# Five small reorderings of banks, copies and products in a chunked-attention and bilinear-FFN kernel

## The chip, the cores and the metric

One core of one Trainium2 chip. The time is the device time of one execution in microseconds (us).

The engines are named as the profile names them: PE (TensorE matmuls), PEld (its weight loads, beside PE), DVE (VectorE), ACT (ScalarE), POOL (GpSimd), and SP, whose queue issues most transfers. A "bank" is one of the PSUM areas into which PE writes; the kernel calls them pa, pb, pc, po, pq and pt.

## The reference, cut to what matters

```python
# q, k, v: 8 batches, 8 heads, 576 rows, 64 columns; attention within chunks of 64 rows
scores = scale * q_c @ k_c.T ; attn = softmax(scores) ; out = attn @ v_c
x = out as [4608 tokens, 512]
a = x @ w_a                       # 512 x 1536
b = x @ w_b
result = (a * b) @ w_out          # 1536 x 512
```

The kernel handles the tokens in 18 units of 256, two to a block of 512. A unit is cast, transposed, scored, summed and multiplied with v; a block of x then goes through the two products and the last one. The two products of blocks 0 and 1, and block 0's last one, are done plainly; all others are done by a scheme with seven products for eight, whose arithmetic the change does not touch.

## The kernel before

The transposes of unit 2 (`U == 2`): q and k get one bank each, and DVE and ACT each copy one half of every bank.

```python
t = [bank() for _ in range(2 if U < 2 else 1)]
tp = [t[i % len(t)]....[:, i] for i in range(2)]
...                                           # 4 transposes into tp[0], 4 into tp[1]
for i in range(2):
    on_dve = i == 0 if U in (0, 2) else w == 0 or U == 1
    cp = nc.vector.tensor_copy if on_dve else nc.scalar.copy
    cp(out=dst[:, i], in_=tp[i]...)
```

Block 0 goes in six pairs of column groups. Unit 2's parts are threaded into pairs 4 and 5:

```python
for i in range(NWP):                          # 6 pairs
    pair.b_of(0, ...)                         # 4 products with w_b, ACT copies the bank
    if i == 5: sums(2, halves=True)           # row sums; ACT: ln, exp(-), twice
    pair.b_of(1, ...)
    if i == 4: transpose_pe(2)
    pair.a_of(0)                              # 4 products with w_a, DVE multiplies
    if i == 4: scores(2)
    if i == 5: values(2)                      # attn @ v, DVE multiplies by 1/sum -> xT
    ...
    pair.a_of(1)
```

Block 1 then goes in half blocks `h()` that alternate between the bank pairs (pa, pc) and (pq, po), with unit 3's values after nine of them:

```python
values(3)          # 2 DVE multiplies
bring(6)
h(8)
...
for p in range(3):
    out_part(0, 2, p, psum_q)                 # third output tile of block 0
```

The tail has the last block's output in two groups (`th` 0 and 1), whose sum C lay in po and pa, and whose last product was cut in two halves:

```python
ends = [OutGroup(NBLK - 1, 0, (psum_t, psum_q, psum_o)),
        OutGroup(NBLK - 1, 1, (psum_t, psum_b, psum_a))]
...
for cols in (slice(0, 128), slice(128, 256)) if end else [slice(0, 256)]:
    for kt in range(HFT):
        nc.tensor.matmul(...)                 # 6 products
    if end:
        nc.vector.tensor_scalar(...)          # evict these columns
        store(..., nc.scalar if cols.start else nc.sync)
```

The softmax here doesn't subtract the row's maximum and nothing guards it: scores larger than these inputs give would overflow.

Of the kernel before, what the change touches and what calls it, by code (L numbers as in the profile page):

```python
# [16 lines left out]
def kernel(  # L17
# [28 lines left out]
    NBLK = NTOK // BLK  # L46
# [20 lines left out]
    psum_b = [psum_b0, psum_b1]  # L67
    psum_c = ctx.enter_context(tc.tile_pool(name="psumc", bufs=1, space=PSUM))
    psum_o = ctx.enter_context(tc.tile_pool(name="psumo", bufs=1, space=PSUM))
    psum_q = ctx.enter_context(tc.tile_pool(name="psumq", bufs=1, space=PSUM))  # L70
    psum_t = ctx.enter_context(tc.tile_pool(name="psumt", bufs=2, space=PSUM))
# [16 lines left out]
    def bank(pool=None):  # L88
        if pool is None:
            pool = spread[0]  # L90
            spread.append(spread.pop(0))
        if pool is psum_b:
            pool = psum_b[0]
            psum_b.append(psum_b.pop(0))
        return pool.tile([128, 512], FP32, name=bank_names[id(pool)])
# [133 lines left out]
    def transpose_pe(U, names="qk"):  # L229
        if U not in qkt:  # L230
            qkt[U] = qkt_pool.tile([128, 2, 2, NKT, 128], BF16, name="qkt")
        for n in names:
            w = "qk".index(n)
            src = raw.pop((n, U))
            t = [bank() for _ in range(2 if U < 2 else 1)]
            tp = [
                t[i % len(t)].bitcast(BF16).rearrange("c (i m p) -> c i m p", i=2, m=NKT)[:, i]
                for i in range(2)
            ]
            for i in range(2):  # L240
                for m in range(NKT):
                    nc.tensor.transpose(
                        tp[i][:, m, :],
                        src[:, i, 2 * m:2 * m + 2, :].rearrange("p j d -> p (j d)"),
                        identity,
                    )
            dst = qkt[U][:, w].rearrange("c g m (p i) -> c i m g p", i=2)
# [3 lines that stand above are left out]
                cp(out=dst[:, i], in_=tp[i].rearrange("c m (g p) -> c m g p", g=2))  # L251
# [17 lines left out]
    late = []  # L269
# [56 lines left out]
                out=rs_of[U][:, c], in_=ln_of[U][:, c], func=AF.Exp, scale=-1.0  # L326
            )

    def values(U, pools=(None, None)):
        E, rs, vr = E_of.pop(U), rs_of.pop(U), raw.pop(("v", U))  # L330
        K, u = divmod(U, 2)
        if u == 0:
            x_tiles[K] = x_pool.tile([128, NKT, BLK], FP16, name="xT")
        av = [bank(p).rearrange("p (m g s) -> p m g s", m=NKT, g=2) for p in pools]
        for m in range(NKT):
            for g in range(2):
                for cl in range(2):
                    for j in range(2):
                        nc.tensor.matmul(  # L339
                            av[cl][j * 64:j * 64 + 64, m, g, :],  # L340
                            vr[cl * 64:cl * 64 + 64, g, 2 * m + j, :],
                            E[cl * 64:cl * 64 + 64, j, m, g, :],
                            start=True,
                            stop=True,
                        )
        for cl in range(2):
            x = x_tiles[K][:, :, 256 * u:256 * u + 256]
            for m in (slice(0, 2), slice(2, 4)) if (U, cl) == (1, 1) else [slice(0, 4)]:
                nc.vector.tensor_tensor(
                    out=x.rearrange("p m (g c s) -> p m g c s", g=2, c=2)[:, m, :, cl, :],  # L350
                    in0=av[cl][:, m],
                    in1=rs[:, cl, m].rearrange("p m (g s) -> p m g s", g=2),
                    op=MULT,
                )

    def slot(s=None, f=None):

        if s is not None and s >= NU:
            s = None
        if f is not None:  # L360
            sums(f)
            inverse(f)
        if s is not None:
            scores(s)
        if f is not None:
            values(f)
# [48 lines left out]
    def ab_half(n, ft, u, t, whole=False):  # L415
        i, o = divmod(ft * 128, WCOL)
        c = slice(0, BLK) if whole else slice(256 * u, 256 * u + 256)
        for kt in range(NKT):
            nc.tensor.matmul(  # L419
                t[:, c],  # L420
                w_ab[n, i][:, kt, o:o + 128],
                x_tiles[0][:, kt, c],
                start=(kt == 0),
                stop=(kt == NKT - 1),
            )

    class Pair:
# [3 lines left out]
            self.fts = (2 * i, 2 * i + 1)  # L431
            self.b, self.b_sb = {}, {}

        def b_of(self, n, halves=(None,)):
            ft = self.fts[n]
            for u in halves:
                if ft not in self.b:
                    self.b[ft] = bank(psum_b)
                ab_half("wb", ft, u, self.b[ft], u is None)
            if halves[-1] == 0:  # L440
                return
            self.b_sb[ft] = c_pool.tile(
                [128, BLK], FP32, name=("b_sb", "u_sb", "v_sb", "c_sb")[ft % 4]
            )
            nc.scalar.copy(out=self.b_sb[ft], in_=self.b[ft])
# [137 lines left out]
    class OutGroup:  # L583
# [20 lines left out]
        def part(self, n, th):  # L604
# [7 lines left out]
            halves = lambda t: t if one else t.rearrange("p (h n) -> p h n", h=2)  # L612
# [7 lines left out]
            if n:  # L620
                s1, s2 = so_of[self.K, "s124"]
            t, a, w = (
                lambda: (self.A, a11, b11),
                lambda: (self.A, a12, b21),
                lambda: (self.B, s2, t2),
                lambda: (self.B, s1, t1),
                lambda: (self.C, s3, t3),
                lambda: (self.B, so_of[self.K, "s4"], b22),
                lambda: (self.C, a22, t4),
            )[n]()  # L630
            c0 = 0 if one else th * 256
            end = n == 6 and one and th == 1
            for cols in (slice(0, 128), slice(128, 256)) if end else [slice(0, 256)]:
                for kt in range(HFT):
                    nc.tensor.matmul(  # L635
                        t[:, c0:c0 + 256][:, cols],
                        a[:, kt, th * 128:th * 128 + 128],
                        w[:, kt, cols],
                        start=n in (0, 4) and first and kt == 0,
                        stop=last and kt == HFT - 1,  # L640
                        skip_group_check=True,
                    )
                if end:
                    nc.vector.tensor_scalar(
                        out=rows(self.o1, cols), in0=self.C[:, cols], scalar1=OUT_SCALE,
                        scalar2=None, op0=MULT,
                    )
                    store(
                        self.K, 1, th, self.o1[:, th], cols, nc.scalar if cols.start else nc.sync
                    )  # L650
# [53 lines left out]
    def out_part(K, tg, part, pool):  # L704
        if part == 0:
            out_ps[K, tg] = bank(pool)
        for ft in range(4 * part, 4 * part + 4):
            nc.tensor.matmul(  # L708
                out_ps[K, tg],
                ab_tiles[K][:, ft, tg * 128:tg * 128 + 128],  # L710
                wo_sb[:, ft],
                start=(ft == 0),
                stop=(ft == NFT - 1),
            )
        if part == 2:
            out_tile(K, tg, out_ps.pop((K, tg)))

    with tc.manual_schedule(
# [75 lines left out]

        for i in range(NWP):
            pair = Pair(i) if i else first
            pair.b_of(0, (None,) if i else (1,))
            if i == 5:
                sums(2, halves=True)
            pair.b_of(1, (None,) if i else (1,))  # L800
            if i == 4:
                transpose_pe(2)
            pair.a_of(0)
            if i == 4:
                scores(2)
            if i == 5:
                values(2)
            if 1 <= i < 5:
                combo()
            pair.a_of(1)  # L810
            if 0 <= i < 5:
                combo()
# [24 lines left out]
        halves = [(ft, u) for u in range(2) for ft in range(NFT)]  # L837

        def h(n=1):
            for _ in range(n):  # L840
                half(*halves.pop(0))
# [14 lines left out]
        h(1)  # L856
        inverse(3, 1)
        h(1)
        values(3)
        bring(6)  # L860
        h(8)
        out_0(0)
        transpose_pe(4)
        h(2)
# [20 lines left out]
        h(1)  # L885
        inverse(5)
        for p in range(3):
            out_part(0, 2, p, psum_q)
        spread[:] = [psum_t]
        values(5)  # L890
        h(1)
# [17 lines left out]
        for K in range(2, NBLK):  # L909
            U = 2 * K + 2  # L910
# [36 lines left out]
        for K in range(2, NBLK):  # L947
# [41 lines left out]
                now.p7()  # L989
                last = now  # L990
        ends = [
            OutGroup(NBLK - 1, 0, (psum_t, psum_q, psum_o)),
            OutGroup(NBLK - 1, 1, (psum_t, psum_b, psum_a)),
        ]
        last.add7()
# [42 lines left out]
```

## Time and profile before

| | before |
|---|---|
| median of 6 runs | 303.72 us (303.65 to 305.45) |
| span in the profile | 301.6 us |
| PE busy | 97% |
| PE's waits that the change aims at | six, 2.3 us by the profile |

The profile lists each engine's waits with what ended them. As PE is the bound, only its own waits matter. They are shown and read in the prediction, which was written from three runs, with a median of 303.73 us.

### The profile page before, as it was taken

What the parts mean: (1) busy time and instruction counts of PE and PEld (TensorE: products, weight loads), DVE (VectorE), ACT (ScalarE), POOL (GpSimd) and SP (SyncE); (2) the same over time, 40 slices, a digit from 0 to 9 for tenths busy, and PEclk for the clock granted to TensorE, in tenths of its full rate; (3) what the DMA queues carried; (4) which work ended last, traced back from release to release, by engine and by line L of the source; (5) the groups of instructions that cost most, each with busy time, mean ns of one, the idle gap of its engine ahead of it and who ended that gap; (6) DMA issues with size and microseconds to landing.
All of it is one profiled execution on the core that took longest, in us unless ns stands there. A gap on an engine that the chain in (4) does not pass through costs nothing.

```text
span 301.6 us, 8619 instructions
## 1 busy us (share of the span) xinstructions
PE 291.5 (97%) x3529; PEld 232.8 (77%) x3531; DVE 213.4 (71%) x344; ACT 197.5 (65%) x358; POOL 192.0 (64%) x179
## 2 busy tenths in 40 slices
PE   6799899999999999999999999999999999999995
PEld 2454468765688888888888888888888888888884
DVE  3548766857977696679667866795679577965773
ACT  2843567358587768776877687767776786566622
POOL 0557668999998299817971797179727902780650
PEclk9999999999999999999999999999999999999999
DMA  7999999999999999899869486947723001100024
GB/s 229 319 381 358 298 306 366 256 206 210 257 243 183 207 194 264 181 214 220 185 155 206 160 183 153 238 134 180 124 67 89 5 2 70 73 3 0 2 106 172
DMA packets 141159, 54.29 MB, mean 180 GB/s; under 512 B 117184, under 2 KB 135232, under 8 KB 141120
## 3 DMA queue, kind: packets, MB, share of 16 engines
q1 hardware_dynamic: 140976, 53.69, 71.0%
q8 instruction: 27, 0.44, 0.6%
q14 instruction: 12, 0.10, 0.1%
q10 hardware_dynamic: 144, 0.07, 0.1%
HBM read 37.75 MB, written 9.44 MB: 156 GB/s over the span
## 4 chain that ended last, share of the span: by engine, by line
PE 90%; ACT 4%; DVE 3%; DMA 2%; issue 1%; SPq 0%; DVEq 0%
PE pb L492 19%; PE pc L492 12%; PE pa L492 12%; PE po L635 12%; PE pq L635 10%; PE pb L419 3%; PE pb L708 3%; PE pa L401 2%; PE po L401 2%; PE pq L401 2%; PE pt L339 2%; PE pt L306 2%; DMA st<-in_k_dram 2%; PE pc L401 2%; PE po L419 1%; PE pc L419 1%
## 5 line engine op out<-in xcount | busy, mean ns | idle before, releaser
L572 POOL TENSOR_TENSOR so<-ab_sb 128x512 f16<-128x512 f16 x23 | 27.6, 1198 | 69.3 <-DVE ab_sb L542 69.3
L492 PEld LDWEIGHTS <-t 128*128 128x128 f16 x504 | 48.3, 98 | 8.5 <-issue 1.7
L492 PE MATMUL pb<-s,wa 128*128 128x256 f16 x336 | 50.5, 273 | 0.0
L492 PE MATMUL pa<-xT,wb 128*128 128x256 f16 x336 | 50.4, 273 | 0.0
L530 DVE TENSOR_TENSOR c_sb<-pc,v_sb 128x512 f32<-128x512 f32 x42 | 28.9, 688 | 26.9 <-ACT v_sb L503 25.6
L635 PEld LDWEIGHTS <-ab_sb 128*128 128x128 f16 x390 | 37.8, 98 | 5.2 <-issue 0.9
L492 PEld LDWEIGHTS <-wb 128*128 128x128 f16 x336 | 32.9, 98 | 4.0
L492 PEld LDWEIGHTS <-wa 128*128 128x128 f16 x336 | 31.8, 98 | 4.2 <-issue 0.2
L542 DVE SCALAR_TENSOR_TENSOR ab_sb<-pc,c_sb 128x512 f16<-128x512 f32 x42 | 29.0, 690 | 7.9 <-PE pc L492 6.5
L503 ACT COPY u_sb<-pb 128x512 f32<-128x512 f32 x42 | 24.7, 588 | 14.8 <-PE pb L492 14.7
L542 DVE SCALAR_TENSOR_TENSOR ab_sb<-pb,b_sb 128x512 f16<-128x512 f32 x42 | 28.9, 689 | 6.1 <-PE pb L492 5.2
L510 ACT COPY pb<-pa 128x512 f32<-128x512 f32 x42 | 24.0, 573 | 10.3 <-PE pa L492 9.9
L635 PEld LDWEIGHTS <-so 128*128 128x128 f16 x288 | 28.1, 98 | 3.4
L503 ACT COPY b_sb<-pa 128x512 f32<-128x512 f32 x42 | 25.0, 595 | 7.1 <-PE pa L492 7.1
L531 DVE TENSOR_TENSOR pc<-pc,u_sb 128x512 f32<-128x512 f32 x42 | 28.9, 688 | 0.0
L572 POOL TENSOR_TENSOR so<-so,ab_sb 128x512 f16<-128x512 f16 x23 | 27.2, 1184 | 1.7
L503 ACT COPY v_sb<-pb 128x512 f32<-128x512 f32 x42 | 24.7, 587 | 5.0 <-PE pb L492 4.4
L572 POOL TENSOR_TENSOR ab_sb<-ab_sb 128x512 f16<-128x512 f16 x23 | 26.8, 1165 | 0.0
L572 POOL TENSOR_TENSOR so<-ab_sb,so 128x512 f16<-128x512 f16 x23 | 26.3, 1174 | 0.0
L492 PE MATMUL pb<-s,t 128*128 128x256 f16 x168 | 25.3, 273 | 0.0
L492 PE MATMUL pc<-xT,t 128*128 128x256 f16 x168 | 25.2, 272 | 0.1
L492 PE MATMUL pc<-s,t 128*128 128x256 f16 x168 | 25.2, 273 | 0.0
(140 smaller groups left out, 570.9 us busy)
## 6 DMA issues: line engine op xcount, KB each, us to landing
st<-in_v_dram SPq DMA_DIRECT2D x32, 256.0 KB, 4.4
out_dram<-o_sb SPq DMA_DIRECT2D x30, 256.0 KB, 2.3
st<-in_k_dram SPq DMA_DIRECT2D x22, 256.0 KB, 4.6
st<-in_q_dram SPq DMA_DIRECT2D x20, 256.0 KB, 3.5
st<-in_q_dram SPq DMA_DIRECT2D x6, 512.0 KB, 6.0
st<-in_moe_w_b_dram SPq DMA_DIRECT2D x6, 512.0 KB, 7.4
st<-in_moe_w_a_dram SPq DMA_DIRECT2D x6, 512.0 KB, 6.7
st<-in_moe_w_out_dram SPq DMA_DIRECT2D x6, 512.0 KB, 6.6
```

Source lines behind the costliest of these rows:

```text
L306: nc.tensor.matmul(sm[cl][j * 64:j * 64 + 64, :], ones[cl * 64:cl * 64 + 64, :], E[cl * 64:cl * 64 + 64, j].rearrange("p m g s -> p (m g s)"),
L401: nc.tensor.matmul(ps[n], w_ab[n, i][:, kt, o:o + 128], xT[:, kt, c0:c1], start=(kt == 0), stop=(kt == NKT - 1),)
L419: nc.tensor.matmul(t[:, c], w_ab[n, i][:, kt, o:o + 128], x_tiles[0][:, kt, c], start=(kt == 0), stop=(kt == NKT - 1),)
L492: nc.tensor.matmul(t[:, h * 256:h * 256 + 256], w[:, kt, h * 128:h * 128 + 128], x[:, kt], start=start and h == 0 and kt == 0, stop=h == 1 ...
L503: nc.scalar.copy(out=t, in_=src)
L510: nc.scalar.copy(out=self.B, in_=self.A)
L530: nc.vector.tensor_tensor(out=self.c, in0=self.C, in1=self.v, op=ADD)
L531: nc.vector.tensor_tensor(out=self.C, in0=self.C, in1=self.u, op=ADD)
L542: nc.vector.scalar_tensor_tensor(out=self.dst[:, :, c0:c0 + 256], in0=t.rearrange("p (h n) -> p h n", h=2), scalar=AB_SCALE, in1=o.rearran ...
L572: (eng or nc.gpsimd).tensor_tensor(out=o, in0=x0, in1=x1, op=op)
L635: nc.tensor.matmul(t[:, c0:c0 + 256][:, cols], a[:, kt, th * 128:th * 128 + 128], w[:, kt, cols], start=n in (0, 4) and first and kt == 0, ...
L708: nc.tensor.matmul(out_ps[K, tg], ab_tiles[K][:, ft, tg * 128:tg * 128 + 128], wo_sb[:, ft], start=(ft == 0), stop=(ft == NFT - 1),)
```

## The change

Five places where PE waits are rearranged; not one product is added or removed. The diff, cut:

```diff
-            t = [bank() for _ in range(2 if U < 2 else 1)]
+            t = [bank() for _ in range(2 if U < 3 else 1)]
...
+            if later is not None and cl == 1:          # in values()
+                later.append(lambda: normalize(slice(0, 4)))
...
-            pair.b_of(0, (None,) if i else (1,))
+            pair.b_of(0, (None,) if i else (1,), i == 5)     # late: no copy yet
...
+            if i == 5:
+                values(2)
+                pair.copy(0)
+                pair.copy(1)
             pair.a_of(0)
...
-        values(3)
+        second = []
+        values(3, later=second)
         bring(6)
-        h(8)
+        h(1)
+        second.pop()()
+        h(7)
...
-            out_part(0, 2, p, psum_q)
+            out_part(0, 2, p, psum_b)
...
-            OutGroup(NBLK - 1, 0, (psum_t, psum_q, psum_o)),
+            OutGroup(NBLK - 1, 0, (psum_t, psum_q, psum_c)),
...
+            for cols in (slice(0, 128), slice(128, 256)) if end else []:
                 if end:                                # evictions after all 12 products
```

More of the change, by code (lines that the diff above doesn't have):

```diff
@@ L327, in inverse, with values @@
             )
-    def values(U, pools=(None, None)):
+    def values(U, pools=(None, None), later=None):
         E, rs, vr = E_of.pop(U), rs_of.pop(U), raw.pop(("v", U))
@@ L347, in values, with normalize @@
             x = x_tiles[K][:, :, 256 * u:256 * u + 256]
-            for m in (slice(0, 2), slice(2, 4)) if (U, cl) == (1, 1) else [slice(0, 4)]:
+            def normalize(m, cl=cl):
                 nc.vector.tensor_tensor(
@@ L354, in values @@
                 )
+            if later is not None and cl == 1:
+                later.append(lambda: normalize(slice(0, 4)))
+            elif (U, cl) == (1, 1):
+                normalize(slice(0, 2))
+                normalize(slice(2, 4))
+            else:
+                normalize(slice(0, 4))
     def slot(s=None, f=None):
@@ L432, in __init__, with b_of @@
             self.b, self.b_sb = {}, {}
-        def b_of(self, n, halves=(None,)):
+        def b_of(self, n, halves=(None,), late=False):
             ft = self.fts[n]
@@ L439, in b_of, with copy @@
                 ab_half("wb", ft, u, self.b[ft], u is None)
-            if halves[-1] == 0:
-                return
+            if halves[-1] != 0 and not late:
+                self.copy(n)
+        def copy(self, n):
+            ft = self.fts[n]
             self.b_sb[ft] = c_pool.tile(
@@ L796 @@
             pair = Pair(i) if i else first
-            pair.b_of(0, (None,) if i else (1,))
+            pair.b_of(0, (None,) if i else (1,), i == 5)
             if i == 5:
                 sums(2, halves=True)
-            pair.b_of(1, (None,) if i else (1,))
+            pair.b_of(1, (None,) if i else (1,), i == 5)
             if i == 4:
                 transpose_pe(2)
+            if i == 5:
+                values(2)
+                pair.copy(0)
+                pair.copy(1)
             pair.a_of(0)
@@ L805 @@
                 scores(2)
-            if i == 5:
-                values(2)
             if 1 <= i < 5:
```

## The prediction

> **What bounds the kernel now.** I read the page first. Its first two parts say that the TensorE is the bound nearly everywhere, at an undisturbed clock.
>
> ```profile
> PE 291.5 (97%) x3529; PEld 232.8 (77%) x3531; DVE 213.4 (71%) x344; ACT 197.5 (65%) x358; POOL 192.0 (64%) x179
> PEclk9999999999999999999999999999999999999999
> PE 90%; ACT 4%; DVE 3%; DMA 2%; issue 1%; SPq 0%; DVEq 0%
> ```
>
> PE is busy for 291.5 of 301.6 us, and 90% of the chain that ended last is PE work. No product is removed by this change, so it can only win where PE stands still. The second view is the list of PE's own waits over the whole span. I leave out those before 18 us, where the first units start and the change touches nothing.
>
> ```profile
> PE pa L279 <- ACT qkt L251: 0.9, 1, 0.9
> ...
> PE pa L635 <- DVE o_sb L644: 0.4, 1, 0.4
> PE pq L401 <- ACT o_sb L699: 0.3, 1, 0.3
> PE pa L401 <- DVE xT L349: 0.3, 1, 0.3
> PE po L635 <- DVE o_sb L676: 0.2, 1, 0.2
> PE po L401 <- DVE ab_sb L410: 0.2, 1, 0.2
> ```
>
> Each of these six occurs once, and each is the target of one edit. Together they are 2.3 us, or 0.8% of 303.73 us. These figures run from one modelled matmul end to the next start, so they understate: a group of four 256-column products issues every 0.44 us but is shown as 0.60 us. I therefore size each stall below from start times. Between 77 and 290 us the list has no PE wait of 0.2 us or more. That matters for whether an early gain survives.
>
> The third view is the timeline at the largest stall, the transposes of unit 2:
>
> ```profile
> 32.54 1.35 DVE L251 COPY qkt<-pt 128x512 bf16<-128x512 bf16 x2 [0.28 <-PE pt L242]
> ...
> 33.31 1.35 ACT L251 COPY qkt<-pt 128x512 bf16<-128x512 bf16 x2 [0.63 <-DVE qkt L251]
> ```
>
> q and k each have one bank, of which DVE copies one half and ACT the other. ACT stood still for 0.63 us until DVE had finished with q's bank, although both only read it. The scores of unit 2 started at 34.71, after ACT's last copy.
>
> **What the Trainium skill says.** "PSUM — Partial Sum Buffer", section "PSUM bank collisions raise a hardware error", says that two engines may not be in one bank and quadrant at once, two readers included, so access is to be guarded by bank. The trace agrees with the effect: the 0.63 us above. For unit 0, which has two banks, DVE's copy ran 7.34 to 8.06 and ACT's 7.52 to 8.25, side by side. In the tail PE likewise waits for DVE's eviction of columns that it doesn't write. The same page, section "Engine vs sequencer instructions", calls the ScalarE and VectorE queues strict FIFO. The three changes of order rest on that, and the trace shows engines standing behind their own earlier work. "Perfetto Trace Analysis", section "Optimizing Tensor Performance", has independent groups rotate through different banks so that eviction overlaps the next matmuls; the moves of unit 0's third output tile and of the tail's C are that advice, and the waits for o_sb at L699 and L676 are its absence.
>
> **The change part by part.**
>
> (1) Two banks for unit 2. PE still makes sixteen transposes and DVE and ACT still make two copies each; only the waiting changes. ACT is busy with u_sb from 32.09 to 32.68. Then its two copies can run back to back, each about 0.63 apart and 0.73 long: 32.65 to about 34.03. DVE is done by about 33.7. The scores then start near 34.07 instead of 34.71: **0.64 us**. The stall does not vanish. PE's previous group (from 32.79, four products at about 0.216 us) has issued by 33.65, so some 0.4 us stays, because ACT does two copies after u_sb.
>
> (2) Unit 2's values ahead of the last a columns, both copies of b later. Before:
>
> ```profile
> 39.27 0.69 DVE L451 SCALAR_TENSOR_TENSOR ab_sb<-pc,v_sb 128x512 f16<-128x512 f32 x1 [2.01 <-PE pc L419]
> 39.87 0.68 DVE L349 TENSOR_TENSOR xT<-pa,ln 128x512 f16<-128x512 f32 x1
> 40.47 0.68 DVE L349 TENSOR_TENSOR xT<-pq,ln 128x512 f16<-128x512 f32 x1
> ```
>
> Block 1's first product started at 41.20, after xT was finished at 41.15. Its weights were loaded at 40.73, so it would have started at about 40.83: a stall of 0.37. After the change, moved up by (1): sums at about 36.25. ACT then makes ln and exp twice without a copy ahead of them, at its present steps of 0.54 to 0.63 from 36.7, done at about 39.1. PE makes the values at about 37.55, and the second multiply ends at about 39.8. PE wants xT at about 40.1. The stall goes: **0.37 us**. The price is off the path if it fits: the copies of b end at about 39.6 and 40.15, DVE's two products with a end at about 40.45 and 41.05, while PE needs those banks (pc, po) back at about 40.5 and 41.4. The first is tight. The v cast of unit 2 ended at 36.61, in time.
>
> (3) Unit 3's second multiply after one more half block. The product into po started at 53.57; the one before started at 52.76 and four of them issue in 0.44, so it was due at 53.20: a stall of 0.37. It waited for DVE's L410 at 53.10, which stood behind both multiplies (51.91 and 52.51, 0.6 each in the queue). With one multiply ahead, L410 ends near 52.9. The second multiply then ends near 53.45, and the first product that reads it, moved up to about 53.63, still finds it ready. Gain **0.37 us**.
>
> (4) Unit 0's third output tile in pb instead of pq. L401 into pq started at 76.15 behind ACT's eviction of pq (75.50 to 76.10); its weight load at 75.77 would have put it at about 75.87: 0.28. But the tile now needs a pb bank, and by the rotation that is the one that unit 4's values free at 72.76 (DVE L349, 72.08 to 72.76); PE was at that tile at 72.72. A new wait of about 0.1 is likely. Net **0.15 to 0.2 us**.
>
> (5) The tail. C in pc is free since 289.13; in po it waited for L676, which DVE reached only at 291.81 behind its combinations. The previous group (from 291.51, six at 0.11) had issued by 292.17, and C started at 292.54: **0.37 us**. Then the last group: its second six products started at 298.04, after the eviction at 297.70, and were followed by their own eviction at 298.57 to 298.86. Without that interleaving all twelve are done about 0.35 after the first six, and the two evictions follow at 0.21 to 0.28 each; the second ends some **0.3 us** earlier. There is a limit: DVE's L683 at 295.29 waited 2.8 us for a store to free its o_sb and does not move. The chain L683, L687 ends at 296.05 and 296.72, against a need of about 296.14 and 296.80. It fits by less than 0.1. Stores also ran near 400 GB/s here. I count 0.55 of 0.67.
>
> Sum: 0.64 + 0.37 + 0.37 + 0.17 + 0.55 = **2.1 us**.
>
> **The rivals.** (a) The early gain is swallowed by a later wait. Transfers are nearly saturated up to about 60 us, POOL waits for them, and an earlier PE could meet an input that doesn't come earlier. For: POOL waited for DMA before most casts around 37 to 42. Against: each cast that I could place has at least 0.5 us to spare (k of unit 3 is cast at 40.08, needed near 41). If it swallowed (1) and (2), the time would be about 302.6. (b) The moved copies on ACT or DVE become PE's new wait, around 40 to 44 or 53 to 54. For: several banks come back within 0.1 us of need. Against: most of these queues shift together with PE. Cost 0.1 to 0.5 us: about 302. (c) The tail is held by its stores: the slot wait at 295.29 is unmoved, and the last eviction is followed by about 2.7 us of store whatever happens. Then the tail gives 0.2 and the sum is 1.8: about 301.95. (d) Everything fits and (1) finds ACT free sooner: at most 2.5, about 301.2.
>
> **Range and chances.** 303.73 less 2.1 is 301.63; I say 301.6. The three runs of before lie within 0.7 us of each other, which alone is a third of the gain. The low end, 300.9, is the full sum with run scatter; the high end, 302.6, is rival (a). A gain of 2% would need 6.1 us, more than all PE waits that the change touches, so faster by over 2% gets 0.01. Slower by over 2% needs a new recurring wait; the code repeated in the middle is only touched in the parity of the pb banks: 0.01.
>
> **What would show it.** In PE's waits the entries for L401 on xT, ab_sb and o_sb, and for L635 on o_sb, should be gone, and that for the scores on qkt should fall to about 0.4. ACT's qkt copies should start right after u_sb, beside DVE's. The first block-1 product should start near 40.1 instead of 41.20. A small new wait in L708 on xT near 71 would show the price of (4). The prediction is wrong if a new PE wait appears after 42 us on a cast or a bank, if the distance from 41.20 to the tail grows, or if the tail's last eviction moves less than the middle does.

## The result, and the profile after

| | before | after |
|---|---|---|
| median of 6 runs each | 303.72 us (303.65 to 305.45) | 302.01 us (301.64 to 302.62) |
| ratio | | 0.9933, 95% interval 0.9908 to 0.9957 |

The ratio is the mean time of one kernel's fast runs over that of the other's of the same rounds, so not quite the ratio of the medians. The change saves 1.7 us by the medians. It is real but below 2%.

The page of the changed kernel, its engines' busy times and the chain's shares:

```profile
PE 291.7 (97%) x3531; PEld 232.9 (77%) x3531; DVE 213.7 (71%) x344; ACT 197.3 (66%) x358; POOL 191.2 (64%) x179
PE 90%; SPq 3%; DMA 2%; DVE 1%; ACT 1%; issue 0%; DVEq 0%
```

PE does the same work. The saving has to be in its waits. Those of the changed kernel, the start-up ones left out (columns: in total, times, longest):

```profile
PE po L339 <- POOL v_raw L224: 1.1, 1, 1.1
...
PE pc L504 <- DVE ab_sb L554: 0.2, 1, 0.2
PE pt L279 <- ACT qkt L251: 0.2, 1, 0.2
```

Of the six waits five are gone, and the one at the scores has shrunk from 0.9 to 0.2. Two are new (the dots hide a third, of 0.2 us on the cast of w_a near 19 us, which belongs to the start). The first, 1.1 us on unit 1's v, ended at 15.34 us, ahead of anything that the change touches; this profile happens to be of the slowest of the six runs. The second, at 109 us, is in a part that neither kernel changes. Both need an explanation.

**The ruler.** Two traces can be laid side by side more exactly than by their wait lists: both kernels make 3531 weight loads, in the same order except in one stretch that the change reorders. So the n-th load's start in one trace less that in the other is how far PE is ahead. A step between two marks is a gain or a loss of that stretch alone. Shift against the one trace of before, in us (negative is earlier); the marks are times in before, the last column is the end of the last transfer's packets:

| kernel | 20.0 (start) | 34.7 (scores) | 41.2 (block 1) | 53.6 (po) | 72.3 | 75.8 (in tile 3) | 76.2 (pq) | 109.1 | 110.4 | 288.1 | 298.0 | last packet |
|---|---|---|---|---|---|---|---|---|---|---|---|---|
| after | +1.11 | +0.37 | -0.05 | -0.42 | -0.47 | -0.38 | -0.75 | -0.76 | -0.43 | -0.54 | -1.46 | -0.76 |
| after_again | +0.42 | -0.33 | -0.74 | -1.11 | -1.17 | -1.07 | -1.43 | -1.44 | -1.44 | -1.45 | -2.36 | -1.66 |
| after_third | +0.14 | -0.61 | -1.03 | -1.40 | -1.46 | -1.15 | -1.52 | -1.52 | -1.52 | -1.51 | -2.43 | -1.70 |
| banks_only | +0.71 | -0.03 | -0.03 | -0.03 | -0.09 | -0.09 | -0.09 | -0.14 | -0.14 | -0.14 | -0.14 | -0.13 |
| values_only | +0.01 | +0.01 | -0.41 | -0.38 | -0.44 | -0.44 | -0.44 | -0.45 | -0.45 | -0.55 | -0.56 | -0.55 |
| third_and_second | +0.26 | +0.25 | +0.25 | -0.13 | -0.18 | -0.09 | -0.46 | -0.46 | -0.46 | -0.77 | -0.77 | -0.76 |
| tail_only | +0.29 | +0.30 | +0.30 | +0.30 | +0.24 | +0.24 | +0.24 | +0.19 | +0.56 | +0.56 | -0.35 | +0.36 |

The rows after the first belong to experiments below. The column "start" holds +1.11, but also +0.29 in tail_only, whose first 280 us are the kernel before. And in all three traces of the changed kernel the shift falls by the same amounts, within 0.02 us, from the start to 72.3 us and again in PE's tail; only the third tile and the wait at 109 us differ.

The same lines as those shown of before, now of the changed kernel. First the transposes' copies:

```profile
33.20 0.58 ACT L457 COPY u_sb<-pb 128x512 f32<-128x512 f32 x1 [0.28 <-PE pb L428]
33.42 0.75 DVE L251 COPY qkt<-pt 128x512 bf16<-128x512 bf16 x1
33.68 0.74 ACT L251 COPY qkt<-pt 128x512 bf16<-128x512 bf16 x1
34.06 0.72 DVE L251 COPY qkt<-pa 128x512 bf16<-128x512 bf16 x1
34.27 0.75 ACT L251 COPY qkt<-pq 128x512 bf16<-128x512 bf16 x1
```

ACT goes straight from u_sb into its copies, and DVE's and ACT's overlap. Next, block 1's first product, before and then after, with the DVE multiply that it reads:

```profile
41.20 0.60 PE L401 MATMUL pa<-xT,wb 128*128 128x256 f16 x4 [0.26 <-DVE xT L349]
```

```profile
40.20 0.69 DVE L350 TENSOR_TENSOR xT<-pt,ln 128x512 f16<-128x512 f32 x1 [0.35 <-ACT ln L325]
...
41.16 0.60 PE L410 MATMUL pa<-xT,wb 128*128 128x256 f16 x4
```

The multiply ends at 40.89, 0.27 ahead of need, and no wait is left. Unit 3's multiplies, with one product into ab_sb let in between them:

```profile
51.86 0.68 DVE L350 TENSOR_TENSOR xT<-pt,ln 128x512 f16<-128x512 f32 x1
52.46 0.41 DVE L419 SCALAR_TENSOR_TENSOR ab_sb<-po,u_sb 128x256 f16<-128x256 f32 x1
52.79 0.68 DVE L350 TENSOR_TENSOR xT<-pb,ln 128x512 f16<-128x512 f32 x1
```

po is free at 52.87 rather than 53.51, and PE's product into it starts on time, at 53.15. That product before, then after:

```profile
53.57 0.60 PE L401 MATMUL po<-xT,wa 128*128 128x256 f16 x4 [0.21 <-DVE ab_sb L410]
```

```profile
53.15 0.60 PE L410 MATMUL po<-xT,wa 128*128 128x256 f16 x4
```

The product into pq behind unit 0's third output tile, before and then after, no longer waits for ACT's eviction of that tile:

```profile
76.15 0.60 PE L401 MATMUL pq<-xT,wb 128*128 128x256 f16 x4 [0.31 <-ACT o_sb L699]
```

```profile
75.40 0.61 PE L410 MATMUL pq<-xT,wb 128*128 128x256 f16 x4
```

The tail, before and then after:

```profile
297.70 0.28 DVE L644 TENSOR_SCALAR o_sb<-pa 128x128 f32<-128x128 f32 x1
298.04 0.49 PE L635 MATMUL pa<-wot,ab_sb 128*128 128x128 f16 x6 [0.38 <-DVE o_sb L644]
...
298.57 0.29 DVE L644 TENSOR_SCALAR o_sb<-pa 128x128 f32<-128x128 f32 x1 [0.59 <-PE pa L635]
298.90 0.37 ACTq L579 DMA_DIRECT2D out_dram<-o_sb  x1
```

```profile
296.25 0.83 PE L647 MATMUL pa<-wot,ab_sb 128*128 128x128 f16 x12
...
297.12 0.49 DVE L657 TENSOR_SCALAR o_sb<-pa 128x128 f32<-128x128 f32 x2 [0.24 <-PE pa L647]
297.64 0.40 ACTq L591 DMA_DIRECT2D out_dram<-o_sb  x1
```

The twelve products run through and the last eviction ends at 297.61 instead of 298.86: 1.25 us earlier. Yet the span ends only 0.8 us earlier. This is the one place where the result does not follow PE.

### The profile page after: what moved, and what is told of

It is laid out like the page before. It is cut to its first block, busy times and chain, and to the rows that moved or that the text cites. A ratio compares the mean times of both kernels' runs of the same rounds, so it can differ in the third digit from the quotient of the medians.

```text
span 300.8 us, 8625 instructions
## 1 busy us (share of the span) xinstructions
PE 291.7 (97%) x3531; PEld 232.9 (77%) x3531; DVE 213.7 (71%) x344; ACT 197.3 (66%) x358; POOL 191.2 (64%) x179
## 4 chain that ended last, share of the span: by engine, by line
PE 90%; SPq 3%; DMA 2%; DVE 1%; ACT 1%; issue 0%; DVEq 0%
PE pb L504 19%; PE pc L504 12%; PE pa L504 12%; PE po L647 12%; PE pq L647 10%; PE pb L721 4%; PE pb L428 3%; DMA st<-in_moe_w_a_dram 2%; PE pq L410 2%; PE pt L339 2%; PE pa L410 2%; PE po L428 2%; PE po L410 2%; PE pc L410 2%; SPq L188 2%; PE pc L428 2%
## 5 line engine op out<-in xcount | busy, mean ns | idle before, releaser
L350 DVE TENSOR_TENSOR xT<-pt,ln 128x512 f16<-128x512 f32 x31 | 20.2, 686 | 8.6 <-PE pt L339 6.6
```

The costliest lines, as they stand in the source:

```text
L350: nc.vector.tensor_tensor(out=x.rearrange("p m (g c s) -> p m g c s", g=2, c=2)[:, m, :, cl, :], in0=av[cl][:, m], in1=rs[:, cl, m].rearra ...
```

## The experiments

Theory: the change is the sum of five independent repairs of PE, each worth what its wait was; the tail's is mostly lost in the stores. Main rivals: an early gain is lost again later; the late start belongs to the change; the tail is held by SP's issuing and not by the transfers.

### Each part alone

banks_only is the kernel before with the one line of the diff about `U < 3`.

> Two banks for unit 2's transposes, nothing else. Theory (bank sharing): ACT's copies start beside DVE's, the stall of PE before the scores of unit 2 falls from 1.16 us beyond the normal step to about 0.45, and PE's first product of block 1 comes 0.7 us earlier; time about 303.0. Rival (the start of the profile of the changed kernel, 1.1 us late, comes with the extra banks): the product that waits for unit 1's v comes near 15.3 instead of 14.2 here too and the time does not fall.

Measured: 303.30 us median, ratio 0.9977 (0.9937 to 1.0017). The table has the step: from +0.71 to -0.03 at the scores, 0.74 us. The product on unit 1's v came at 14.58 us, 0.41 later than before and not near the rival's 15.3; the 0.71 includes a later wait. The 0.74 us is still there at 288 us: nothing swallows it. The time alone could not have told this, as its interval includes 1. (The 1.16 us in the expectation, and the figures of this stall below, count about 0.1 us more than the prediction's reckoning, which lets the products before it issue every 0.216 us: by that it was 1.06 us, 33.65 to 34.71. The differences are the same.)

values_only has the diff's lines in the pair loop and `b_of`/`copy`, on single banks.

> Unit 2's values ahead of the last a columns and the two copies of b after, on the single bank. Theory: the stall of 0.36 us before block 1's first product goes, the stall of 1.16 us before the scores stays; time about 303.3. Rival (gain needs the earlier scores, because ACT is late): some 0.2 us of stall stays there.

Measured: 304.08 us median, ratio 1.0005 (0.9958 to 1.0052); the profiled run was 302.81. The stretch from the scores to block 1 gains 0.42 us and the stall at the scores stays at 1.16. So this part does not need the other. The time shows nothing: its four runs spread over 1.8 us.

third_and_second has the later second multiply and the third tile in pb.

> Only unit 3's later second multiply and unit 0's third output tile in pb. Theory: the stalls of 0.37 us at po near 53.6 and 0.39 us at pq near 76.2 both go, a new one of 0.1 us stands at the third tile near 72.7; PE is 0.65 us earlier at 80 us; time about 303.1. Rival: the second multiply comes too late for the first product that reads it, 0.1 to 0.3 us of new stall near 54.

Measured: 303.15 us median, ratio 0.9970 (0.9930 to 1.0010). A gain of 0.38 us at po, a loss of 0.09 and a gain of 0.37 at the third tile and pq: as expected. No wait near 54. The shift grows by another 0.3 us between 124 and 214 us, in steps of 0.1 to 0.2 once per block; what makes these is left open.

tail_only has the last two parts of the diff.

> Only the tail: C in pc, and the last two groups of six without an eviction between them. Theory: PE ends 0.7 us earlier but the last store lands only 0.2 to 0.3 us earlier, because SP's queue is still issuing the store before and the stores then take longer; time about 303.4. Rival (stores hidden, as half of the prediction's sum assumed): the last store moves with the last eviction, 0.6 to 0.7 us; time about 303.05.

Measured: 303.79 us median, ratio 0.9989 (0.9952 to 1.0026). From 288 to 298 us PE gains 0.91 us, the last packet only 0.20 (from +0.56 to +0.36). The theory's number, not the rival's. This kernel also shows the wait at 109 us (from +0.19 to +0.56), although it is the kernel before in that place: that wait does not belong to the change. Its start is 0.29 us later than that of the one trace of before, so the start too varies without the change, but not by 1.1 us here.

### The changed kernel again

> The changed kernel once more. Theory (start is luck of the first transfers): PE's first product on unit 1's values comes anywhere between 13.9 and 15.4 us, as it did in kernels whose start is unchanged, and from there to the end the gains are as before: 1.16 us at the scores and block 1, 0.38 at po, 0.27 net at the third tile, 0.9 in PE's tail. Rival (the change delays the start): again near 15.3. The wait of 0.33 us at the product into pc near 109 us may or may not come back: it stood in the changed kernel and in the one with the tail alone, not in three others.

Measured: 302.04 us, ratio 0.9924 (0.9886 to 0.9963). The start is at +0.42, with the product on unit 1's v at 14.56 us, and there is no wait at 109 us. All steps repeat: gains of 0.75, 0.41, 0.37, a loss of 0.10 and a gain of 0.36 at the third tile, 0.91 in PE's tail, 0.21 in the last packet.

The rival's 15.3 did not come. Whether a smaller part of the late start belongs to the change is not settled by this. Up to 26 us the weight loads, the instructions of DVE, ACT and POOL and the transfers are the same, in the same order, in all thirteen traces. Yet the eight traces with two banks for unit 2 have the product on unit 1's v at 14.21 to 15.34 us, the five without at 13.92 to 14.54. So a link is unlikely and not excluded; what makes v late was not tested.

### Is it the shared bank?

one_bank_per_engine leaves each of q and k a single bank, but no bank has two readers:

```diff
-                on_dve = i == 0 if U in (0, 2) else w == 0 or U == 1
+                on_dve = i == 0 if U == 0 else w == 0 or U == 1
```

> The kernel before, with unit 2's q bank copied by DVE alone and its k bank by ACT alone: one bank each, no bank read by two engines. Theory (the 0.63 us were the bank's): ACT's two copies start when k's transposes are done, scores 0.4 to 0.5 us earlier than in the kernel before, stall beyond the normal step down from 1.16 to about 0.7. Rival (a second bank is what counts, for PE's transposes): scores not earlier.

Measured: one run of 303.96 us. DVE takes both halves of q, ACT both of k, and they overlap:

```profile
33.35 1.34 DVE L251 COPY qkt<-pt 128x512 bf16<-128x512 bf16 x2
33.80 1.33 ACT L251 COPY qkt<-pt 128x512 bf16<-128x512 bf16 x2 [0.31 <-PE pt L242]
```

The step from the start to the scores is 0.34 us (from +0.81 to +0.47), somewhat below the 0.4 to 0.5 expected, and the stall falls from 1.16 to 0.83. Without a second bank, only by giving each bank one reader, nearly half of the 0.74 us comes. The rest is the start: counted from the first transpose of unit 2, ACT began its two copies at 1.42 us and ended them at 2.77 in the kernel before, 1.10 and 2.43 here (first transpose at 32.70), 0.68 and 2.02 in the changed kernel (33.00). With two banks ACT can begin on q while k is still being transposed; here its first bank is k's.

### What holds the tail?

tail_store_on_act moves one more store to ACT's queue, so that two of the last three go by it:

```diff
                     store(self.K, 1, c, self.o1[:, c], lo if one else slice(0, DM),
+                        nc.scalar if one else nc.sync)
```

> The changed kernel with the store of the last but one group (lower columns of th 0) and the last half issued by ACT's queue, so that SP is free for the first half. Theory A (SP's issue is the tail's bound): the last store is issued 0.3 us earlier and its last packet lands 0.3 us earlier against PE's end. Theory B (the transfers themselves are the bound): the issue moves, the last packet does not, within 0.1 us.

tail_early_store sends the lower columns of o0 as soon as they are evicted, and the upper ones by ACT's queue:

```diff
+                if one:                         # after o0's first eviction
+                    store(self.K, 0, th, self.o0[:, th], lo)
...
-                    store(self.K, 0, c, self.o0[:, c])
+                    store(self.K, 0, c, self.o0[:, c], hi if one else slice(0, DM),
+                          nc.scalar if one else nc.sync)
```

> The changed kernel with the lower columns of o0 stored right after their eviction (two stores of 128 KB moved from about 296 to about 291 us) and the upper ones issued by ACT. Theory B (transfers bound the end): the last packet comes 0.4 to 0.5 us earlier against PE's last product, 1.2 us after its issue as in the kernel before, unless the early stores delay the o_sb that DVE waits for near 294.7, which would push PE's last groups by up to 0.3. Theory A: only what the issue gives, 0.3.

Measured, one run each: 302.29 and 302.75 us (the latter with its start at +1.73). By the ends in their traces:

| kernel | last product's end to last packet | issue of the last store to last packet |
|---|---|---|
| before | 1.57 us | 1.21 us |
| after, after_again, after_third | 2.27, 2.27, 2.30 | 1.62 in after |
| tail_store_on_act | 2.31 | 1.75 |
| tail_early_store | 1.77 | 1.21 |

tail_store_on_act alone was no test of theory A. Of the last two stores one was issued 0.36 us after PE's last product instead of 0.65, but the other, which needs the second eviction, stayed at 0.56. So the last issue moved by 0.09 us and not by 0.3, and the last packet not at all. What decides is tail_early_store beside it: the last two stores are issued at the same 0.36 and 0.56 us after PE's last product, but 256 KB have gone earlier, and the last packet comes 0.54 us earlier (1.77 instead of 2.31). That is theory B. The transfers show why. Rate of the DMA engines in GB/s in 40 slices of 0.075 us, first before (from 298.1 us), then after (from 297.1), then tail_early_store (from 297.8):

```profile
GB/s 437 437 382 383 410 355 355 437 437 410 410 382 328 369 410 369 341 342 335 280 116 7 96 294 321 144 21 0 0 0 0 0 0 0 0 0 0 0 0 0
```

```profile
GB/s 41 273 410 437 410 355 410 437 437 383 410 437 382 410 328 410 437 410 328 355 369 410 348 349 321 342 335 328 171 34 0 0 0 0 0 0 0 0 0 0
```

```profile
GB/s 314 123 191 314 423 396 314 110 14 164 355 410 396 301 110 14 102 280 328 280 307 294 137 21 0 0 0 0 0 0 0 0 0 0 0 0 0 0 0 0
```

In the kernel before the stores ran near 400 GB/s until the dip to 7, and the last one came into an empty pipe. In the changed kernel there is no dip: the last store is ready before its predecessors are through. With 256 KB sent early the dips are back, and the last store takes 1.21 us again. So of the 0.7 us that PE gained and the end did not (2.27 less 1.57), 0.5 was waiting in the transfers, and an earlier store brings it out. The other 0.2 is the last issue: 0.56 us after PE's last product in tail_early_store, 0.36 in the kernel before.

### The wait at 109 us

POOL's cast of unit 9's v and DVE's first combination for block 3 start within 0.11 us of each other in all eleven traces with the cast in this place. The two in the kernel before, in the changed kernel and in its repetition:

```profile
107.84 0.41 DVE L472 TENSOR_TENSOR s<-xT 128x512 f16<-128x512 f16 x1
107.84 1.31 POOL L224 CAST v_raw<-st 128x1024 bf16<-128x1024 f32 x1
```

```profile
107.09 1.04 POOL L224 CAST v_raw<-st 128x1024 bf16<-128x1024 f32 x1
107.14 1.27 DVE L484 TENSOR_TENSOR s<-xT 128x512 f16<-128x512 f16 x1
...
109.06 0.60 PE L504 MATMUL pc<-s,t 128*128 128x256 f16 x4 [0.17 <-DVE ab_sb L554]
```

```profile
106.40 1.31 POOL L224 CAST v_raw<-st 128x1024 bf16<-128x1024 f32 x1
106.41 0.41 DVE L484 TENSOR_TENSOR s<-xT 128x512 f16<-128x512 f16 x1
```

One of them is always held up by the other. If it is DVE's, the multiply behind it in DVE's queue frees pc late, and PE waits about 0.3 us. "SBUF — State Buffer", section "Who interferes with whom", of the Trainium skill says that a DVE instruction with two SBUF inputs contends with a GpSimd instruction that reads SBUF; these durations agree. To test it, one line:

```diff
-                if K == 2 and i == 4:
+                if K == 2 and i == 5:
                     cast(9, "v")
```

> The changed kernel with POOL's cast of unit 9's v one stage later, so that it no longer starts at the same moment as DVE's first combination for block 3 near 107 us. In ten runs of both kernels so far the one that came first held up the other: five times the combination took 0.41 us and the cast 1.31, five times 1.2 to 1.3 and 1.04, and in exactly these five PE waited 0.27 to 0.38 us at a product into pc near 109. Theory: the combination takes 0.41 us and PE's wait near 109 is gone. Rival (the multiply is late for another reason): the wait stays at about 0.3.

Measured: one run of 301.95 us. The combination took 0.42 us and the wait is not there. Over the eleven traces with the cast in its old place, DVE came through first six times, POOL five, in both kernels, and PE waited in exactly those five. The start times do not tell which: DVE's combination started 0.002 us ahead of the cast in the kernel before and in one_bank_per_engine, and took 0.41 us in the one and 1.3 in the other.

### A version that combines them

The changed kernel with the later cast, the early store, and `pair.copy(1)` of pair 4 after the transposes; after_third is the changed kernel unaltered, in the same rounds.

> The changed kernel with three additions: the later cast of unit 9's v, the early store of o0's lower columns, and ACT's copy of the second b of pair 4 after the transposes' copies instead of ahead of them. Theory: the stall before the scores of unit 2 falls from 0.42 to about 0.1 to 0.2, none near 109, the last packet 0.5 earlier against PE's end; 0.8 us under the changed kernel on average, near 301.2. Rival (DVE is then the later of the two at the scores, and the copies of b come late for the product after): the stall stays near 0.4 and the gain is 0.6 or less.

> The changed kernel beside the combined one, for their comparison in the same rounds: near 302.0, ratio to the kernel before 0.992 to 0.995.

Measured: combined 301.69 us (300.89 to 302.39), ratio to before 0.9914 (0.9887 to 0.9940); the changed kernel 302.25 us (301.66 to 303.20), 0.9936 (0.9911 to 0.9962). Both beat the kernel before. The combined one is 0.6 us below the changed one by the medians, short of the 0.8 expected, and the intervals overlap, so these times don't settle it. But the six runs fall into two groups: 302.23 to 302.39 at a mean granted clock of 0.994, and 300.89 to 301.15 at 1.000. The profile is of the first group. Its stretch from 14 to 20 us, and the same of after_third (columns: stretch, length, busy us of PE, PEld, DVE, ACT, POOL with instructions, granted clock, DMA share, GB/s):

```profile
14.00:20.00 6.00, 5.23 (x58) 3.16 (x56) 2.35 (x5) 2.66 (x5) 2.72 (x3) 0.72 1.05 361
```

```profile
14.00:20.00 6.00, 5.70 (x66) 3.30 (x66) 3.10 (x6) 3.42 (x6) 2.27 (x4) 1.00 1.07 371
```

The granted clock was 0.72 there. Runs with such a dip are some 1.3 us longer (302.36 less 301.01, the groups' medians), and it comes in the kernel before as well: 7 of 25 runs in the three sets of timed runs had a mean clock of 0.992 to 0.994, at 304.81 to 305.95 us, median 305.20, the other 18 had 0.998 or more at 303.24 to 304.92, median 303.71. Of the changed kernel's 16 runs with their clocks known one had the dip (303.20); the other 15 have a median of 302.19. Run against run without the dip the combined version, at 301.01 in three runs, is 1.2 us below the changed kernel and 2.7 below the kernel before. This sorting was made after the runs and on three of them, so it is a strong hint and no verdict. What sets off the dip was not examined.

The traces confirm two of its parts (1.77 us from last product to last packet, no wait at 109 us) and refute the third: the stall at the scores stays at 0.41. The rival had that number, but for another reason (DVE as the later of the two): ACT was still the later, and, freed of u_sb, it waited for the transposes themselves. In after_third the tile in pb cost 0.31 us instead of 0.10; see below.

## Why the prediction was right or wrong

The time, 302.01 us, is within the range of 300.9 to 302.6, and the mechanism held for each part. By its own steps, with the three traces of the changed kernel:

| step | predicted, us | measured, us |
|---|---|---|
| (1) two banks | 0.64 | 0.74, 0.75, 0.75 |
| (2) values ahead | 0.37 | 0.42, 0.41, 0.42 |
| (3) second multiply | 0.37 | 0.37, 0.37, 0.37 |
| (4) third tile, net | 0.15 to 0.2 | 0.28, 0.26, 0.06 |
| (5) tail, at the last packet | 0.55 | 0.22, 0.21, 0.19 |

**Steps (1) to (3)** were right to about 0.1 us. The stall that stays at the scores was put at 0.4 and is 0.32 by the same reckoning (34.76 to 35.08 in the changed kernel). The two tight banks of (2), pc and po, came back in time. The 0.74 of (1) is not fixed, though. Three more traces are the changed kernel up to that place: tail_store_on_act has 0.74, but cast9_later and tail_early_store have 0.56 and 0.57. There a DVE combination shortly ahead of its two copies started 0.05 to 0.07 us behind a POOL cast and took 1.25 and 1.27 us, against 0.77 to 0.94 in the three of the table, and DVE's copies ended last instead of ACT's. It has the look of the wait at 109 us; no run tests it here.

**Step (4)** was right in both terms, a gain and a new wait for unit 4's multiply in pb, but the size of the new wait is not fixed: 0.10 us twice and 0.31 once. In after_third PE was due at the tile at 71.26 and that multiply ended at 71.52; in the profile of the result they stood at 72.24 and 72.29. In after_third DVE's combination two places ahead of the multiply had started 0.10 us behind a POOL cast and took 1.21 us, against 0.45 in the profile of the result.

**Step (5)** is the term that was mis-sized: "I count 0.55 of 0.67". Up to the last eviction the sum of 0.67 was right: it ended 1.25 us earlier, and PE was already 0.54 us ahead at 288 us, which leaves 0.71. (PE itself gained 0.92 us: 0.38 at C and 0.54 at the second six products, which no longer wait for an eviction.) The margin that was feared (o_sb freed in time for L683) held. What failed is the discount: the transfers were full and the last store was issued later against PE's end, so that an eviction 0.7 us earlier moved the last packet by 0.2. Rival (c) had this number. It was named for the slot wait and for some 2.7 us of store after the last eviction "whatever happens"; those became 3.2 us (297.61 to the span's end at 300.82), and most of the cause was the third thing, noted in the text only in passing: stores near 400 GB/s.

The measured steps add up to 2.0 us, 1.8 where (4) came out low, against the 2.1 of the sum: small errors of (1), (2) and (4) made good most of that of (5). That the sum came out so close is luck. The medians differ by 1.7. What remains is no larger than the effects that come and go from run to run in both kernels: the start, which differed by up to 1.8 us between traces, with unit 1's v and the clock's dip, and the 0.3 us at 109. A start that is later with the change, not excluded above, would be part of it too. Over all runs without the dip (those of the section before) the medians differ by 1.5 us and the means, 303.88 and 302.06, by 1.8. How the other two were spread over the timed runs can't be told, as only one run of each set has a trace.

**Rival (a)** fell: from 41 to 288 us no stretch gives back what (1) and (2) gained, in the traces without the wait at 109 us. **Rival (b)** fell for the moved copies; a wait of its kind, at 109 us, is in both kernels.

## What to carry to other kernels

Where one engine is the bound, line up two traces by the n-th instruction of that engine: steps of 0.1 us show, where times that scatter by a per cent show nothing. At the end of a kernel ask what the last store finds ahead of it: work that ends earlier only helps if the stores before it are already through, so send parts of the output as soon as they exist. When a bank is borrowed to end one wait, look who last used it; its release is the new wait.

## What the Trainium skill lacked or had wrong

- "SBUF — State Buffer", section "Who interferes with whom", lists that such a DVE instruction and a POOL cast contend, and the runs agree: a two-input combination behind a cast was held until about the cast's end (1.2 to 1.3 us instead of 0.41), and the cast behind it took 1.31 instead of 1.04. What it lacks is that with starts within 0.11 us of each other the order was not the program's to choose: six of eleven traces one way, five the other, 0.3 us of PE apart.
- "Perfetto Trace Analysis", section "Optimizing Tensor Performance", advises rotating through banks and doesn't warn that a borrowed bank brings the wait of its last user: 0.10 to 0.31 us at the third tile.
- "DMA: Bandwidth & Descriptors", section "Latency and other measured facts", says that a lighter HBM load makes the fixed cost of a transfer smaller; these runs do not separate that from waiting behind other stores. It gives no figure for the case that decided here, the last store of a burst. 64 KB took 1.21 us from issue to the last packet when the pipe had emptied, 1.62 to 1.75 behind stores at some 400 GB/s.
